# K(4) loaded among the weights of a DeltaNet and SwiGLU kernel, and five smaller edits

## The chip, the cores and the metric

The kernel runs on one core of a Trainium2 chip. The metric is the device time of one execution in microseconds (us). The kernel before was run three times: 692.01, 693.07 and 694.98 us, with the median at 693.07. Engines are named as in the profile: PE is TensorE, PEld its weight loads, DVE is VectorE, ACT is ScalarE, POOL is GpSimd, and SP is the engine that issues most DMAs.

## What is computed

Two blocks, one behind the other. The first is a delta rule over 768 time steps for 4 batches of 8 heads with head dimension 48; the second is a SwiGLU feed-forward block over the 3,072 resulting tokens:

```python
k_n = k / (np.linalg.norm(k, axis=-1, keepdims=True) + 1e-06)
for t in range(S):
    y[:, :, t] = np.einsum('bhd,bhde->bhe', q[:, :, t], state)
    v_old = np.einsum('bhde,bhd->bhe', state, kt)
    state = state + bt[:, :, :, None] * np.einsum('bhd,bhe->bhde', kt, vt - v_old)
...
g = x @ w_gate                      # 384 x 1536
silu = g * (1.0 / (1.0 + np.exp(-g)))
out = (silu * (x @ w_val)) @ w_out  # 1536 x 384
```

Queries, keys, values and beta are 32-bit floats; the three weight matrices come as 64-bit floats and are made 32-bit ones on the chip.

## The kernel before

**Chunks.** Time is cut into 12 chunks of 64 steps. Within a chunk the recurrence becomes matrix products: Gram products of the keys, a triangular inverse, products with the state, and a new state. `advance(c)` is a generator that takes chunk c through these in steps; each `next` issues one step on all engines. The result of a chunk is transposed into `xts[c]`, the 256 tokens that the feed-forward block reads. For chunk 0 the last steps are y (products of L1175, copies L1184 to L1192), x (transposes L1206, copies L1209 and L1210) and the state (`of_state`, L1145).

**Keys, queries, values.** K(c), q(c) and v(c) are the loads of one chunk, each 384 KB in 192-byte runs: two DMAs for K and q (L140), four for v (L186). There are four buffers for keys, so K(4) reuses that of K(0) and is issued at the end of chunk 0's state step (`rows_freed_by`). There are two buffers each for q and v. `turned` transposes keys or queries on TensorE (L511) and copies them back on ScalarE; `gram_steps` (L527) makes the Gram products. `products(4, 2)` does both for K(4) and q(2), with unread products ahead of them (`small_unread`, L658: tiny products whose result nobody reads).

**Weights.** They come in 42 pieces. Pieces 0 to 23 have 256 columns (256 KB, gate and value in turn: even numbers are gate), 24 to 29 have 512 columns (512 KB), 30 to 41 are rows of the output weight (384 KB). `stage(n, after)` issues the load of a piece on SP (L260) into a place that is borrowed from buffers not yet in use; for the early ones a one-element GpSimd copy (L259) holds it until the piece three numbers earlier has landed. A later piece is staged as soon as the piece whose place it takes has been converted (`freed_by`). A piece goes through two ScalarE instructions (`power_step`, L272 and L278) and three on VectorE (`convert`: L289, L297, L309); `convert(ns, ahead)` also runs the powers of some pieces ahead. Each engine works in program order, so a power whose piece has not landed holds all ScalarE work behind it.

**Order.** The whole schedule is by hand: each engine's queue is in the order of the program text. In the first part the pairs (c, f) for the chunks c = 0 and 1 and the column blocks f = 0, 2, ..., 10 go in this order: (0,0), (0,2), (0,4), (0,6), (1,0), (1,2), (1,4), (1,6), (0,8), (1,8), (0,10), (1,10). `gate_val(c, f)` makes the gate product (12 matmul records of L1409), its silu (ACT L1418), the value product and their product h (DVE L1420). The gate and the value product have one PSUM bank each of four, in turn. During (0,0) and (0,2) `chain(at)` is called behind each quarter: it takes a step of `advance` of chunk 0 or 1 and converts one or two pieces. From (0,4) on `fill` converts pieces behind the silu and behind h, and `point` puts in other chunk work: ahead of (0,4) the transposes of K(4) and q(2), ahead of (0,6) their Gram products, whose copies are L553 and L556 on ScalarE. At (1,0) the inverse of the second pair of chunks starts (L856, L569, L860). From chunk 2 on a faster scheme with fewer products runs to the end.

On SP the order around the change is: pieces 18 to 22, q(2), v(2), K(4), piece 23, piece 29, v(3), piece 24, K(5), pieces 25, 26, 28, 27.

Of the kernel before, what the change touches and what calls it, by code (L numbers as in the profile page):

```python
# [20 lines left out]
def kernel(  # L21
# [25 lines left out]
    nc = tc.nc  # L47
# [4 lines left out]
    NB = B // 2  # L52
# [97 lines left out]
    def load_q(c):  # L150
        load_heads(qpad[c % QB], q, c)
# [28 lines left out]
    def load_v(c):  # L180
        vin[c] = work.tile([128, 2, NB, NJ, D], FP32, name="vin", bufs=2)
        for b in range(2):
            src = halves(v, c, b).rearrange("bp (j par) p d -> par p (bp j) d", par=2)
            for par in range(2):
                s = 64 * (b ^ par)
                nc.sync.dma_start(  # L186
                    out=vin[c][s : s + 64, par].rearrange("p bp j d -> p (bp j) d"),
                    in_=src[par],
                )
# [87 lines left out]
        )  # L277
        nc.scalar.activation(power, words_of[:, :, 0], ACTF.Copy, scale=2.0**-29)  # L278

    def convert(ns, ahead=6):  # L280

        work_of = []
        for n in ns:
            dst, _, t, f0, m = pieces[n]
            power_step(n)
            place = staged.pop(n)[:, 0:m]
            work_of.append((dst[:, t, f0 : f0 + m].bitcast(U32), place, powers.pop(n)))
        for dst, place, _ in work_of:
            nc.vector.tensor_scalar(  # L289
                out=place,  # L290
                in0=dst,
                scalar1=3,
                scalar2=None,
                op0=ALU.logical_shift_left,
            )
        for dst, place, _ in work_of:
            nc.vector.scalar_tensor_tensor(  # L297
                out=dst,
                in0=dst,
                scalar=0x80000000,  # L300
                in1=place,
                op0=ALU.bitwise_and,
                op1=ALU.bitwise_or,
            )
        for n in range(ns[-1] + 1, ns[-1] + 1 + ahead):
            if n < min(N_HALF, len(pieces)) or ns[-1] + 3 > n < len(pieces):
                power_step(n)
        for dst, _, power in work_of:
            nc.vector.tensor_tensor(out=dst, in0=dst, in1=power, op=ALU.add)  # L309
        for n in ns:  # L310
            for later in freed_by.get(n, ()):
                stage(later)
# [635 lines left out]
    def advance(c):  # L948
# [100 lines left out]
                skip_group_check=True,  # L1049
            )  # L1050
        if c == 0:
            nc.vector.tensor_copy(v0[:, 0], p_u[:, 0])
            nc.scalar.copy(v0[:, 1], p_u[:, 1])
        elif c == 1:
            flat = v0.rearrange("p par bp j d -> p (par bp j d)")
            for bank in range(2):
                p = p_u_of[bank].rearrange("p par j d -> p par (j d)")
                nc.scalar.copy(by_bank(flat, bank), p)
            v_flat = qpad[1].rearrange("p bp h d -> p (bp h d)")[:, 0 : HH * D]
            v1 = v_flat.rearrange("p (par bp j d) -> p par bp j d", par=2, bp=NB, j=NJ)  # L1060
            crossed_copies(other_half(v_flat), other_half(flat))
            nc.scalar.copy(v1[:, :, 0], v0[:, :, 0])
        else:
            nc.scalar.copy(v0, p_u)
# [54 lines left out]
                    if n + par < 3:  # L1119
                        yield MORE  # L1120
        if c + 2 < NCH:
            if c < 2:
                load_v(c + 2)
            else:
                late_loads.append(lambda: load_v(c + 2))
        yield
        pq = p_sb.pop(c)
# [78 lines left out]
                nc.tensor.transpose(p, y_f[:, bp, at], ident)  # L1206
        x_v = xts[c].rearrange("p t (bp n) -> p t bp n", bp=NB)
        if c == 0:
            nc.scalar.copy(x_v[:, :, 0], p_f[0])  # L1209
            nc.vector.tensor_copy(x_v[:, :, 1], p_f[1])  # L1210
        else:
            nc.scalar.copy(x_v, p_f)
        if 2 <= c < NCH - 1 and (c + 1) // 2 in n_t:
# [400 lines left out]

    todo = list(range(len(pieces)))

    def converts(n):
        if todo:
            convert(todo[:n])
            del todo[:n]  # L1620

    def converts_first(*ns):
# [20 lines left out]
    def products(k_c, q_c):  # L1643

        if k_c == AHEAD:
            small_unread(40)
        if k_c is not None:
            turned(k_c, False)
        if q_c is not None:
            turned(q_c, True)  # L1650
        yield
        if k_c is not None:
            gram(k_c, False, None, (nc.scalar.copy, nc.scalar.copy))
            if k_c % 2 == 1:
                fills.append((k_c // 2, invert(k_c // 2)))
        if q_c is not None and q_c < MERGED:
            gram(q_c, True)
        yield
# [103 lines left out]
    with tc.manual_schedule(  # L1762
# [16 lines left out]
        load_q(1)  # L1779
        load_v(0)  # L1780
        copy_a = nc.scalar.copy
        small_unread(48)
        unread(2)
        turned(0, False, 0)
        p_g = [first_gram(0, "px")]
# [33 lines left out]
        first_z()  # L1819
        some, others = slice(0, HH // 2), slice(HH // 2, HH)  # L1820
        spread_z(0, 1, nc.scalar, some)
        for n in range(18, 23):
            stage(n, n - 3)
        load_q(QB)
        spread_z(0, 0, nc.vector)
        spread_z(0, 1, nc.vector, others)
        scale_v(0)
# [5 lines left out]
        next(first_q[1])  # L1833
        for x in range(2):
            spread_z(1, x, nc.scalar)
        for n in (2, 4, 1, 3, 5, 6, 7):
            power_step(n)
        for _ in range(6):
            step("advance", advance, 0)
        converts_first(0)  # L1840
        step("advance", advance, 0)
        converts_first(2)
        p_n = banks("p_n", "px")
        n_products(1, p_n, (0,))
# [4 lines left out]
        converts_first(5)  # L1849
        scale_v(1)  # L1850
        n_copies_1(p_n, zb_1.rearrange("p k i -> p (k i)"))

        def chain(at):

            step("advance", advance, 0 if steps("advance", 0) < 4 else 1)
            converts((1, 2, 2, 1)[at])

        pairs = [(c, f) for c in range(2) for f in range(0, 8, 2)]
        pairs += [(c, f) for f in range(8, FT, 2) for c in range(2)]
# [65 lines left out]
```

## Time and profile before

| | us |
|---|---|
| median of three runs | 693.07 |
| the profiled execution | 694.12 |
| its span, first to last instruction | 692.4 |
| PE busy | 675.3 |
| DVE busy | 414.2 |
| ACT busy | 262.9 |
| POOL busy | 193.1 |

The page cuts the span into 40 slices of 17.3 us and gives the busy share of each engine in tenths (9 is 90% or more), the clock that TensorE was granted, and the share of the DMA engines:

```
PE   8897999999999999999999999999999999999997
DVE  7898489798666765647456546655555534433342
ACT  4785576213543533344323245232143242142230
PEclk9999899999999999999999999999999999999999
DMA  9667925007561621464333364243243221221210
```

The first four slices hold the loads, the first chunks and the first columns of the weights; from the fifth on TensorE is full. In the timelines below, a row has the start and the length in us, engine, line, operation, tiles and count, and in brackets the idle time before it and what ended it. A row can stand for several instructions, and its length then reaches from the first start to the last end.

### The profile page before, as it was taken

The page shows a single profiled execution, that of the slowest core. Times are in us where ns is not written, and L with a number is a line of the kernel's source. Part 1 is how long each engine was busy: PE and PEld are TensorE (multiplying, and loading weights), DVE is VectorE, ACT ScalarE, POOL GpSimd, SP SyncE. Part 2 cuts the span into 40 slices and gives each one's busy share as a digit, 9 for nine tenths or more (in the row PEclk, how much of TensorE's full clock was granted, in tenths as well). Part 3 has the DMA queues.
Part 4 walks back from the last instruction along what each step waited for, and adds up shares of the span by engine and source line. Part 5 has one row for each costly group of instructions (what it writes and reads, how often), then busy time and mean ns, then how long its engine had stood idle before and what let it go on. Part 6 is the DMA issues. An engine that isn't in the chain of part 4 may idle for free.

```text
span 692.4 us, 24603 instructions
## 1 busy us (share of the span) xinstructions
PE 675.3 (98%) x10836; PEld 630.0 (91%) x10836; DVE 414.2 (60%) x874; ACT 262.9 (38%) x557; POOL 193.1 (28%) x310
## 2 busy tenths in 40 slices
PE   8897999999999999999999999999999999999997
PEld 4786888756999999999999999999999999999997
DVE  7898489798666765647456546655555534433342
ACT  4785576213543533344323245232143242142230
POOL 5110031105893037820037830208810000000000
PEclk9999899999999999999999999999999999999999
DMA  9667925007561621464333364243243221221210
GB/s 133 160 177 180 257 69 161 1 24 163 134 121 25 114 81 40 97 113 93 78 87 71 70 128 81 55 97 83 55 109 69 56 63 47 55 62 46 70 46 24
DMA packets 143850, 62.24 MB, mean 90 GB/s; under 512 B 122976, under 2 KB 126048, under 8 KB 143744
## 3 DMA queue, kind: packets, MB, share of 16 engines
q1 hardware_dynamic: 141536, 60.19, 37.6%
q8 instruction: 85, 1.39, 0.9%
q10 hardware_dynamic: 2080, 0.39, 0.4%
q14 instruction: 21, 0.17, 0.1%
q0 software_dynamic: 128, 0.10, 0.1%
HBM read 53.58 MB, written 7.08 MB: 88 GB/s over the span
## 4 chain that ended last, share of the span: by engine, by line
PE 91%; DVE 3%; ACT 2%; DMA 2%; issue 1%; SPq 0%; DVEq 0%; ACTq 0%
PE ffn L1313 42%; PE ffn L1519 20%; PE ffn L1409 9%; PE ffn L1436 4%; DMA kn<-in_k_dram 2%; PE p_px L977 2%; PE p_py L960 2%; PE p_px L1043 2%; PE p_py L1133 2%; PE p_px L1145 1%; PE p_px L527 1%; PE p_py L1206 1%; PE ffn L1072 1%; PE p_px L921 1%; PE p_py L935 1%
## 5 line engine op out<-in xcount | busy, mean ns | idle before, releaser
L1313 PE MATMUL ffn<-x_ffn,wg_sb 128*128 128x128 f32 x840 | 128.5, 276 | 0.5 <-ACT ffn L1369 0.3
L1313 PE MATMUL ffn<-x_ffn,wv_sb 128*128 128x128 f32 x840 | 128.2, 275 | 0.0
L1313 PEld LDWEIGHTS ffn<-x_ffn,wg_sb 128*128 128x128 f32 x840 | 111.1, 192 | 1.0 <-ACT ffn L1369 0.7
L1313 PEld LDWEIGHTS ffn<-x_ffn,wv_sb 128*128 128x128 f32 x840 | 110.7, 192 | 0.0
L1348 DVE TENSOR_TENSOR h_f<-sil,ffn 128x256 f32<-128x256 f32 x120 | 49.7, 418 | 83.2 <-ACT sil L1343 81.8
L1343 ACT ACTIVATE sil<-ffn 128x256 f32<-128x256 f32 x120 | 45.8, 383 | 128.5 <-PE ffn L1313 126.4
L1519 PE MATMUL ffn<-wo_sb,h_f 128*128 128x192 f32 x480 | 83.4, 328 | 0.0
L860 POOL TENSOR_TENSOR n_b<-mb,half 128x32 f32<-128x32 f32 x5 | 30.0, 6006 | 183.6 <-DVE mb L569 183.6
L1519 PEld LDWEIGHTS ffn<-wo_sb,h_f 128*128 128x128 f32 x480 | 78.1, 190 | 0.3
L599 POOL TENSOR_TENSOR tmp<-zb,mb 128x31 f32<-128x31 f32 (+15 forms) x124 | 68.6, 553 | 16.9 <-DVE mb L586 7.5
L605 POOL TENSOR_TENSOR zb<-zb,tmp 128x31 f32<-128x31 f32 (+15 forms) x124 | 70.0, 565 | 9.7
L1480 DVE TENSOR_TENSOR ffn<-ffn,p_sb 128x512 f32<-128x512 f32 x58 | 40.4, 696 | 49.1 <-ACT ffn L1369 47.7
L1313 PE MATMUL ffn<-x_t,h_f 128*128 128x128 f32 x480 | 61.0, 280 | 0.2 <-ACT ffn L1326 0.2
L1313 PEld LDWEIGHTS ffn<-x_t,h_f 128*128 128x128 f32 x480 | 56.3, 192 | 2.1 <-ACT ffn L1326 0.3
L1480 DVE TENSOR_TENSOR o_sb<-o_sb,ffn 128x192 f32<-128x192 f32 x49 | 17.2, 352 | 64.1 <-PE ffn L1519 61.5
L1326 ACT COPY ffn<-ffn 128x512 f32<-128x512 f32 x30 | 17.1, 571 | 60.8 <-PE ffn L1313 60.8
L1477 DVE TENSOR_TENSOR h_f<-h_f,h_f 128x256 f32<-128x256 f32 x60 | 29.4, 493 | 11.8 <-PE ffn L1519 10.5
L1519 PE MATMUL ffn<-last_k,h_f 128*128 128x192 f32 x200 | 36.0, 327 | 0.0
L1409 PE MATMUL ffn<-x_ffn,wg_sb 128*128 128x256 f32 x144 | 34.4, 385 | 0.3 <-DVE x_ffn L1210 0.3
L1409 PE MATMUL ffn<-x_ffn,wv_sb 128*128 128x256 f32 x144 | 33.8, 382 | 0.0
L1519 PEld LDWEIGHTS ffn<-last_k,h_f 128*128 128x128 f32 x200 | 32.9, 190 | 0.1
L1409 PEld LDWEIGHTS ffn<-x_ffn,wg_sb 128*128 128x128 f32 x144 | 26.7, 191 | 4.6 <-DVE wg_sb L309 0.8
(323 smaller groups left out, 1123.9 us busy)
## 6 DMA issues: line engine op xcount, KB each, us to landing
h_f<-w_s SPq DMA_DIRECT2D x60, 256.0 KB, 2.8
p_sb<-w_s SPq DMA_DIRECT2D x27, 256.0 KB, 2.8
vin<-in_v_dram SPq DMA_DIRECT2D x48, 96.0 KB, 3.4
out_dram<-o_sb SPq DMA_DIRECT2D x48, 96.0 KB, 2.2
kn<-in_k_dram SPq DMA_DIRECT2D x20, 192.0 KB, 4.6
zt<-in_moe_w_out_dram SPq DMA_DIRECT2D x6, 384.0 KB, 3.9
qpad<-in_q_dram SPq DMA_DIRECT2D x36, 64.0 KB, 3.3
w_s<-h_f SPq DMA_DIRECT2D x7, 256.0 KB, 3.5
```

Source lines behind the costliest of these rows:

```text
L599: engine.tensor_tensor(out=t_v, in0=zb[:, 0 : j + 1, j : j + 1].to_broadcast([128, j + 1, m]), in1=mb[:, j : j + 1, j + 1 : R].to_broadcas ...
L605: engine.tensor_tensor(out=zb[:, 0 : j + 1, j + 1 : R], in0=zb[:, 0 : j + 1, j + 1 : R], in1=t_v, op=ALU.add,)
L860: nc.gpsimd.tensor_tensor(out=n, in0=mb.rearrange("p j i -> p (j i)")[:, 0 : R * R : R + 1], in1=half, op=ALU.pow,)
L1313: nc.tensor.matmul(p[:, u], w(u), moving, start=start and u == 0, stop=True, skip_group_check=True,)
L1326: nc.scalar.copy(p_y, p_x)
L1343: nc.scalar.activation(sil[:, n].rearrange("p (i n) -> p i n", i=2), p[:, 0:2], ACTF.Silu)
L1348: nc.vector.tensor_tensor(out=h_of(c, f, j), in0=sil[:, n].rearrange("p (i n) -> p i n", i=2), in1=p[:, 2:4], op=ALU.mult,)
L1409: nc.tensor.matmul(ps[name][:, i], w_sb[:, t, (f + i) * 128 : (f + i + 1) * 128], xts[c][:, t], start=(t == 0 and i == 0), stop=(t == KT - 1),
L1436: nc.tensor.matmul(p_o, hs[c, f - f % 2][:, f % 2, bp * 128 : (bp + 1) * 128], wo_sb[:, f], start=(f == 0), stop=(f == FT - 1),)
L1477: nc.vector.tensor_tensor(out=out, in0=a, in1=b, op=ALU.subtract)
L1480: nc.vector.tensor_tensor(out=out, in0=a, in1=b, op=ALU.add)
L1519: nc.tensor.matmul(p[x, part], a(f - f % 2)[:, f % 2], b(f), start=not begun and f == 0, stop=f == FH - 1, skip_group_check=True,)
```

## The change

K(4) comes directly behind piece 19 on SP: the loads of pieces 20, 21, 22 and q(2) move from the text ahead of chunk 0's steps into the first `chain` call, behind the state step that issues K(4). v(2) is loaded together with v(3), at chunk 1's step. Nine of the 40 unread products ahead of K(4)'s transposes go to the head of the kernel (48 become 57). The first copy of chunk 0's u, on VectorE, is cut into two halves; both copies of chunk 0's x are on ScalarE, where one was on VectorE. The powers of pieces 6 and 7 are issued later, the addition of piece 0 stands behind the y step, and `chain` runs ahead over other numbers of pieces (`CHAIN`: pieces to convert, pieces ahead).

```diff
-    def convert(ns, ahead=6):
+    def convert(ns, ahead=6, between=None):
...
+        if between is not None:
+            between()
         for n in range(ns[-1] + 1, ns[-1] + 1 + ahead):
...
         if c == 0:
-            nc.vector.tensor_copy(v0[:, 0], p_u[:, 0])
+            for bp in range(NB):
+                nc.vector.tensor_copy(v0[:, 0, bp], p_u[:, 0, bp])
             nc.scalar.copy(v0[:, 1], p_u[:, 1])
...
         if c + 2 < NCH:
-            if c < 2:
-                load_v(c + 2)
-            else:
+            if c == 1:
+                load_v(2)
+                load_v(3)
+            elif c > 1:
                 late_loads.append(lambda: load_v(c + 2))
...
         if c == 0:
-            nc.scalar.copy(x_v[:, :, 0], p_f[0])
-            nc.vector.tensor_copy(x_v[:, :, 1], p_f[1])
+            for bp in range(NB):
+                nc.scalar.copy(x_v[:, :, bp], p_f[bp])
...
-    def converts(n):
+    def converts(n, ahead=6):
         if todo:
-            convert(todo[:n])
+            convert(todo[:n], ahead)
             del todo[:n]
...
         if k_c == AHEAD:
-            small_unread(40)
+            small_unread(31)
...
-        small_unread(48)
+        small_unread(57)
...
-        for n in range(18, 23):
+        for n in range(18, 20):
             stage(n, n - 3)
-        load_q(QB)
...
-        for n in (2, 4, 1, 3, 5, 6, 7):
+        for n in (2, 4, 1, 3, 5):
             power_step(n)
         for _ in range(6):
             step("advance", advance, 0)
-        converts_first(0)
-        step("advance", advance, 0)
+        convert([0], 0, lambda: step("advance", advance, 0))
+        todo.remove(0)
+        power_step(6)
         converts_first(2)
...
         n_copies_1(p_n, zb_1.rearrange("p k i -> p (k i)"))
+        power_step(7)
+
+        later_pieces = list(range(20, 23))
+
+        CHAIN = [(1, 5), (2, 3), (2, 6), (1, 6)] + [(n, 6) for n in (1, 2, 2, 1)]
 
         def chain(at):
 
             step("advance", advance, 0 if steps("advance", 0) < 4 else 1)
-            converts((1, 2, 2, 1)[at])
+            if later_pieces:
+                for n in later_pieces:
+                    stage(n, n - 3)
+                later_pieces.clear()
+                load_q(QB)
+            converts(*CHAIN.pop(0))
```

## The prediction

> **What bounds the kernel now.** I read the page first, then the chain of waits for the first 110 us, then the granted clock by stretches, and last the timelines of single engines.
>
> ```profile
> PE 675.3 (98%) x10836; PEld 630.0 (91%) x10836; DVE 414.2 (60%) x874; ACT 262.9 (38%) x557; POOL 193.1 (28%) x310
> ...
> PE 91%; DVE 3%; ACT 2%; DMA 2%; issue 1%; SPq 0%; DVEq 0%; ACTq 0%
> ```
>
> TensorE is busy 98% of the span and holds 91% of the chain that ended last. Only what keeps TensorE waiting, or what it does without need, can move the end. The chain names one DMA, with 2%. In the order of time (start, length, what), with the stretch around it:
>
> ```profile
> 43.52 1.12 PE p_px L1145 x64
> ...
> 62.08 1.51 PE ffn L1409 x6
> 63.59 0.55 SPq L140
> ...
> 64.18 6.36 DMA kn<-in_k_dram
> ...
> 70.67 1.94 PE p_px L511 x8
> ...
> 74.25 5.18 PE ffn L1409 x24
> ...
> 82.56 27.46 PE ffn L1409 x126
> ```
>
> Here K(4), the fifth chunk's keys, lands at 70.54, and the transposes of L511 wait for it. From 82.56 to 110.02 TensorE then has one unbroken run. What the wait costs beside the idle time shows in the stretches (PE, PEld, DVE, ACT, POOL busy; granted clock; DMA share; GB/s):
>
> ```profile
> 65.70:67.20 1.50, 0.00 (x1) 0.00 (x0) 1.28 (x6) 0.10 (x1) 0.00 (x0) 1.00 0.69 131
> 67.20:70.67 3.47, 0.00 (x0) 0.03 (x1) 1.61 (x5) 0.00 (x0) 0.00 (x0) 0.50 1.05 287
> 70.67:74.05 3.38, 3.38 (x16) 3.38 (x17) 0.00 (x0) 1.83 (x4) 0.00 (x0) 0.50 0.59 85
> 74.05:80.00 5.95, 5.95 (x67) 5.06 (x69) 0.46 (x1) 2.79 (x5) 0.00 (x0) 1.00 1.11 259
> ```
>
> TensorE is idle from 65.70 to 70.67, 4.97 us, and 1.5 us into it the clock drops to half until 74.05. The two sets of transposes take 3.4 us in that stretch.
>
> **The change: K(4) moved.** SP's timeline (start, time on the queue, what):
>
> ```profile
> 52.47 0.38 SPq L260 DMA_DIRECT2D wo_sb<-in_moe_w_val_dram  x1
> 52.94 0.38 SPq L260 DMA_DIRECT2D zt<-in_moe_w_gate_dram  x1
> ...
> 58.25 1.32 SPq L140 DMA_DIRECT2D qpad<-in_q_dram  x2
> 59.68 2.97 SPq L186 DMA_DIRECT2D vin<-in_v_dram  x4
> 62.77 2.24 SPq L140 DMA_DIRECT2D kn<-in_k_dram  x2
> 65.13 0.64 SPq L260 DMA_DIRECT2D zt<-in_moe_w_val_dram  x1
> ...
> 66.64 3.69 SPq L186 DMA_DIRECT2D vin<-in_v_dram  x4
> 70.44 3.00 SPq L260 DMA_DIRECT2D wo_sb<-in_moe_w_gate_dram  x1
> ...
> 74.95 1.63 SPq L260 DMA_DIRECT2D wo_sb<-in_moe_w_val_dram  x1
> ```
>
> The row at 52.47 is piece 19, 52.94 piece 20, then 21 and 22, q(2), v(2), K(4), piece 23, (29), v(3), 24, (K(5)) and 25. Afterwards the order is 19, K(4), 20, 21, 22, q(2), 23, 29, v(2), v(3), 24, K(5), 25. K(4) needs the state product of chunk 0 (L1145, done at 44.64), so nothing holds it after 52.85. With its own 2.24 us of issue and the 6.36 us of its slow second half it would land near 60.5, and with twice that transfer at 67; the transposes want it at 65.4 (below). I take 60.5: hidden. GpSimd's one-element copies for 20 to 22 keep their order. These three pieces move by about 1.5 us on SP's queue; they are converted only behind 66.1, so this lies in cover.
>
> How early TensorE could then be, from its own rows:
>
> ```profile
> 17.16 1.04 PE L511 MATMUL p_py<-ident,kn 128*128 128x128 f32 x8
> 18.04 1.04 PE L511 MATMUL p_px<-ident,last_k 128*128 128x128 f32 x8
> ...
> 64.51 0.30 PE L658 MATMUL p_px<-half 32*32 32x1 f32 x16
> 65.00 0.70 PE L658 MATMUL p_px<-half 32*32 32x1 f32 x64 [0.19 <-issue]
> ...
> 74.09 2.75 PE L1409 MATMUL ffn<-x_ffn,wg_sb 128*128 128x256 f32 x12
> ```
>
> The 40 unread products run from 64.51 to 65.70, 1.19 us; 31 of them take 0.92, to 65.43. The two sets of transposes at full clock take 0.88 and 1.04 us (the rows of 17.16 and 18.04), so with 0.1 us between them and the next products the gate product of (0, 4) starts at 65.43 + 1.92 + 0.1 = 67.4 in place of 74.09: **6.7 us earlier**. It is 4.97 idle, 1.4 of half clock and 0.3 of unread products. It needs q(2) by 66.3; issued at about 58.25 as before, it has 8 us, and K(4)'s slow half took 6.36, so I count no wait.
>
> **What is late next.** Everything behind is not a matter of TensorE alone. Piece 25 (issued at 74.95) took
>
> ```profile
> wo_sb<-in_moe_w_val_dram SPq DMA_DIRECT2D x1, 512.0 KB, 5.6
> ```
>
> from issue to landing, and ScalarE stood waiting for it. The rows that follow, on ScalarE, VectorE and TensorE:
>
> ```profile
> 80.54 0.71 ACT L272 ACTIVATE wv_sb<-wo_sb 128x512 f32<-128x512 f32 x1 [1.94 <-DMA wo_sb<-in_moe_w_val_dram]
> ...
> 84.59 0.60 ACT L1418 ACTIVATE sil<-ffn 128x512 f32<-128x512 f32 x1 [0.19 <-PE ffn L1409]
> ...
> 92.45 0.60 ACT L1418 ACTIVATE sil<-ffn 128x512 f32<-128x512 f32 x1
> ```
>
> ```profile
> 96.36 0.68 DVE L1420 TENSOR_TENSOR h_f<-sil,ffn 128x512 f32<-128x512 f32 x1
> ```
>
> ```profile
> 97.34 2.75 PE L1409 MATMUL ffn<-x_ffn,wg_sb 128*128 128x256 f32 x12
> ```
>
> ```profile
> 84.59:92.45 7.86, 7.86 (x38) 6.92 (x37) 4.93 (x9) 7.82 (x9) 0.00 (x0) 1.00 0.16 63
> ```
>
> On ScalarE the power of piece 25 stands ahead of the Gram copies of chunk 4 and of the silu of (0, 6) at 84.59; from there ScalarE is full until the silu of (1, 0) at 92.45 (the last row: ACT, the fourth engine, 7.82 of 7.86); VectorE then transposes, converts piece 27 and makes h of (1, 0), done at 97.04. The product at 97.34, (1, 4), reuses the PSUM banks that this h frees: four banks, two to each (chunk, f). So TensorE starts (1, 4) only 0.30 us after the other engines have let it, and ScalarE waited 0.19 on the way. Of this 0.49 I count 0.4 as room, the rest as semaphores. The gain at (1, 4) is thus the smaller of 6.7 and 0.4 + (80.54 − the new landing of piece 25).
>
> When does piece 25 land? Up to it SP has to issue the same 3,712 KB from q(2) on less K(4)'s 384. Bound from the slow side: only K(4)'s place on the queue goes (62.77 to 65.13, 2.36 us) and all else keeps its pace, so 78.2 and a gain of 2.8. Below that: a later landing than 80.5 would need the queues to get slower, and v(2) and v(3) back to back could do that (a rival). Bound from the fast side: the 3,328 KB left go at the 259 GB/s of the stretch from 74.05, 13.2 us from 58.25, so 71.4, and the full 6.7 us come. The rows between: three issues were held by full queues, the four of v(3) by 3.69 − 2.97 = 0.7, piece 24 by 2.7 (0.3 to 0.4 is normal in the rows of 52.47 and 52.94), piece 25 by 1.3. Those holds come from the same transfers behind one another, which stay except for K(4). I let a quarter of the 4.7 go: 78.2 − 1.2 = 77.0, nearer the slow bound since that stretch is the same one. **Gain 0.4 + 3.5 = 3.9 us**; TensorE waits 2.8 us ahead of (1, 4). Behind it all engines stand as they stood at 97.34, and the rest of the span keeps its length.
>
> **The small edits.**
>
> ```profile
> 1.03 1.57 PE L658 MATMUL p_px<-half 32*32 32x1 f32 x96 [1.03 <-DVE half L316]
> 9.07 1.06 PE L511 MATMUL ffn<-ident,kn 128*128 128x128 f32 x8 [0.59 <-DMA kn<-in_k_dram]
> ```
>
> ```profile
> 31.35 1.28 DVE L545 TENSOR_TENSOR p_sb<-ffn,mask_q 128x512 f32<-128x512 f32 x2
> 32.75 0.55 DVE L1480 TENSOR_TENSOR uu<-v,ffn 128x384 f32<-128x384 f32 x1
> ...
> 41.09 0.55 DVE L1210 COPY x_ffn<-ffn 128x384 f32<-128x384 f32 x1
> ```
>
> Nine unread products at the head: 48 of them are 96 rows and 1.57 us, so 0.29 us, hidden by the 0.59 us that TensorE waits for K(1) at 9.07; with that cover gone, 0.29. Splitting chunk 0's first copy lets TensorE begin up to 0.3 us sooner, but the first sum at 32.75 starts as soon as the two masks (31.35 and 1.28 long) are through VectorE, so the round trip keeps its pace: 0, at worst 0.16 of a second instruction. The second x copy off VectorE (41.09, 0.55) lets the first gate product begin some 0.5 us sooner, but its third weight still needs its conversion, now shorter by the copy and longer by the addition moved behind the y copies (0.42): 0.2 us for TensorE. The powers issued later stay on ScalarE in full. These 0.2 us, and any wait for q(2) up to 2.8 us, end in the wait ahead of (1, 4) and are worth nothing in the forecast.
>
> **Sum.** The profiled execution took 694.12 us (692.4 span, 1.7 around it), 1.05 above the median of the runs, 693.07. 694.12 − 3.9 = 690.2; the same step from the median gives **689.2 us**.
>
> **The rivals.**
> *The full step*: the DMA queues drain faster without K(4) in the thick of them, piece 25 lands by 74.2, and nothing holds (1, 4): 693.07 − 6.7 = 686.4. For it: the DMA share of only 0.69 in the stretch from 65.70, with K(4) under way. Against: the three holds from 66.64 on, which have other transfers as their cause.
> *No gain*: holds grow as v(2) and v(3) follow one another with four issues each, and piece 25 lands within 1 us of 80.5; the idle time moves from the transposes to (1, 4): 692.5. For it: all bytes ahead of piece 25 are the same ones. Against: issues at 52.94 and 58.25 are 5.3 us apart with two pieces between them, room that K(4) now fills.
> *The clock drops again*: the 2.8 us wait ahead of (1, 4) halves the clock, as 1.5 us of idling after small products did at 67.20. One stretch of 3.4 us with TensorE busy at half clock costs 1.7: 689.2 + 1.7 = 690.9. Against: here the wait stands behind dense products. The Trainium skill (TensorE: Matmul & The Clock Gate, section What's actually happening) has the clock fall only after at least one idle window of about 3.4 us. By that rule a 2.8 us wait leaves the clock alone; the row at 67.20, where it fell after 1.5 us without products, disagrees with a strict reading, so I keep the case.
> *Slower*: one mechanism, piece 25 behind v(2) and v(3). If eight head transfers in a row fill the queues so that piece 25 lands later than 80.9, TensorE waits at (1, 4) longer than it gained. At 83 that is 2.1 us, and the idle time there, 8.8 us, takes the clock with it, 1.7: 696.9. For it: v(3) and piece 24 together sat 6.7 us on SP already. Against: 384 KB fewer ahead of it since q(2).
>
> **How the numbers follow.** Forecast 0.50 (its own range 687.5 to 690.5, piece 25 between 75.4 and 78.4), full step 0.21, no gain 0.14, clock 0.10, slower 0.05. The range of 8 in 10 reaches from below the full step, 685.8 (0.6 for the spread of the runs), to 692.0, leaving out most of the no-gain and slower cases. A measurement of this kernel tells about 0.5%, 3.5 us, from no change. Faster by more than this, under 689.6: the full step and some 0.36 of the forecast's 0.50: 0.57. Slower by more, 0.05. Within: 0.38.
>
> **What would show it.** K(4) lands before 62, TensorE is not idle between 65 and 67, and the granted clock stays at 1.00 there. The gate product of (0, 4) starts near 67.4. ScalarE waits for piece 25 until about 77, and TensorE is idle some 3 us ahead of (1, 4), near 91 to 94, with h of (1, 0) as its releaser. No idle there means the full step; a landing of piece 25 at 80 means no gain. I am wrong altogether if K(4) still holds L511, or if the wait stands at another place, as with q(2).

## The result, and the profile after

| | before | after |
|---|---|---|
| median of 21 runs each, taken together, us | 693.38 | 691.60 |
| lowest and highest | 691.11 to 695.66 | 689.67 to 694.45 |
| the profiled execution | 694.12 | 691.6 |
| its span | 692.4 | 689.9 |

The ratio of the times is 0.9968, with a 95% interval of 0.9957 to 0.9979: the kernel after is faster by 0.32%, some 2.2 us (the two medians of the table differ by 1.78 us, 0.26%, inside that interval). The 691.60 lies in the predicted range, 2.4 us above the forecast of 689.2, and it is less than the 0.5% that the prediction had as the likeliest class.

From the page of the kernel after, TensorE's busy time, and the chain that ended last by engine:

```profile
PE 673.6 (98%) x10836; PEld 627.9 (91%) x10836; DVE 414.3 (60%) x874; ACT 263.6 (38%) x558; POOL 193.9 (28%) x310
...
PE 87%; ACT 5%; DMA 3%; DVE 2%; issue 2%; SPq 1%; POOL 0%; DVEq 0%; ACTq 0%; POOLq 0%
```

TensorE still bounds it, but its share of the chain went from 91 to 87%, and ScalarE's from 2 to 5%. TensorE's busy time fell by 1.7 us (675.3 to 673.6), which is about what half a clock costs over the 3.38 us of transposes at 70.67 in the kernel before (an estimate: half of 3.38). The three stretches that held K(4)'s wait, in the kernel after (PE, PEld, DVE, ACT, POOL busy; granted clock; DMA share; GB/s):

```profile
65.70:67.20 1.50, 1.50 (x71) 1.35 (x70) 1.24 (x5) 1.19 (x3) 0.00 (x0) 1.00 0.98 310
67.20:70.67 3.47, 3.47 (x24) 3.19 (x22) 2.26 (x8) 2.43 (x6) 0.00 (x0) 1.00 0.76 139
70.67:74.05 3.38, 3.38 (x48) 2.76 (x49) 0.35 (x1) 0.60 (x1) 0.00 (x0) 1.00 0.87 162
```

TensorE is busy throughout and at full clock, where it was idle for 4.97 us and at half clock for 6.8. Next, TensorE's timeline after, at the places to compare, and then the list of all its waits between 60 and 125 us (what waited, for what; us in total, times, longest):

```profile
66.45 1.09 PE L513 MATMUL p_px<-ident,kn 128*128 128x128 f32 x8
...
68.25 2.75 PE L1413 MATMUL ffn<-x_ffn,wg_sb 128*128 128x256 f32 x12
...
78.02 1.99 PE L1413 MATMUL ffn<-x_ffn,wg_sb 128*128 128x256 f32 x8 [1.34 <-DVE wg_sb L311]
...
92.80 2.75 PE L1413 MATMUL ffn<-x_ffn,wg_sb 128*128 128x256 f32 x12
96.44 2.86 PE L1413 MATMUL ffn<-x_ffn,wv_sb 128*128 128x256 f32 x12 [0.89 <-DVE h_f L1424]
...
110.71 2.86 PE L1413 MATMUL ffn<-x_ffn,wg_sb 128*128 128x256 f32 x12 [1.05 <-ACT sil L1422]
```

```profile
PE ffn L1413 <- DVE wg_sb L311: 1.3, 1, 1.3
PE ffn L1413 <- ACT sil L1422: 1.1, 1, 1.1
PE ffn L1413 <- DVE h_f L1424: 0.9, 1, 0.9
PE p_py L1210 <- issue: 0.5, 1, 0.5
```

K(4)'s transposes (66.45) wait for nothing. The gate product of (0, 4) starts at 68.25 in place of 74.09, 5.84 us earlier. Then the lead melts in three waits that the kernel before did not have: 1.34 us inside the gate product of (0, 6), 0.89 ahead of the value product of (1, 4), and 1.05 ahead of the gate product of (1, 8). The same products before and after give the ledger:

| product | before | after | lead, us |
|---|---|---|---|
| gate (0, 4) | 74.09 | 68.25 | 5.84 |
| gate (1, 0) | 86.98 | 82.44 | 4.54 |
| gate (1, 4) | 97.34 | 92.80 | 4.54 |
| value (1, 4) | 99.93 | 96.44 | 3.49 |
| gate (1, 8) | 112.88 | 110.71 | 2.17 |
| end of the span | 692.4 | 689.9 | 2.5 |

From 117 to 400 us the lead stays at 2.1; the last 0.4 come near 400 us and were not followed up. The three waits have their releasers on ScalarE and VectorE, here on ScalarE (first four rows) and VectorE (last two) of the kernel after:

```profile
76.30 0.66 ACT L272 ACTIVATE wg_sb<-wo_sb 128x512 f32<-128x512 f32 x1 [4.66 <-DMA wo_sb<-in_moe_w_gate_dram]
...
80.11 0.66 ACT L272 ACTIVATE wv_sb<-wo_sb 128x512 f32<-128x512 f32 x1 [2.60 <-DMA wo_sb<-in_moe_w_val_dram]
...
91.79 0.60 ACT L1422 ACTIVATE sil<-ffn 128x512 f32<-128x512 f32 x1
...
109.19 0.55 ACT L272 ACTIVATE wo_sb<-staged 128x384 f32<-128x384 f32 x1 [2.08 <-DMA staged<-in_moe_w_out_dram]
```

```profile
77.54 0.42 DVE L311 CUSTOM_DVE_ANT_0 wg_sb<-wg_sb,last_h 128x512 uint16<-128x512 uint16 x1 [1.20 <-ACT last_h L278]
...
95.71 0.68 DVE L1424 TENSOR_TENSOR h_f<-sil,ffn 128x512 f32<-128x512 f32 x1
```

ScalarE stands 4.66 us for piece 24 and 2.60 us for piece 25, which landed at 80.09. Behind 80.11 it is full again up to the silu of (1, 0) at 91.79; h of (1, 0) follows at 95.71, and the value product of (1, 4) starts 0.05 us after it ends. The wait at (0, 6) is another path from piece 24: the addition of piece 22 on VectorE (77.54) stands behind a power in `last_h` that ScalarE issued after the load of piece 24. The one at (1, 8) is a silu that stood behind the power of an output-weight piece (109.19). So all three are ScalarE work in program order behind a load that is late. The loads of pieces 24 and 25 are late for what SP had to issue ahead of them (its timeline after; 56.30 is piece 20, 60.88 piece 23, 62.63 piece 29):

```profile
54.89 1.32 SPq L140 DMA_DIRECT2D kn<-in_k_dram  x2
56.30 0.87 SPq L260 DMA_DIRECT2D zt<-in_moe_w_gate_dram  x1
...
59.45 1.32 SPq L140 DMA_DIRECT2D qpad<-in_q_dram  x2
60.88 1.71 SPq L260 DMA_DIRECT2D zt<-in_moe_w_val_dram  x1
62.63 1.48 SPq L260 DMA_DIRECT2D p_sb<-in_moe_w_val_dram  x1
64.17 6.72 SPq L186 DMA_DIRECT2D vin<-in_v_dram  x8
71.00 0.56 SPq L260 DMA_DIRECT2D wo_sb<-in_moe_w_gate_dram  x1
...
73.08 2.89 SPq L260 DMA_DIRECT2D wo_sb<-in_moe_w_val_dram  x1
```

v(2) and v(3) take 6.72 us of the queue in one piece, and piece 24 follows. Piece 25 was issued at 73.08 in place of 74.95, but stood 2.89 us on the queue, not 1.63, and landed only 0.42 earlier (80.51 before). The load behind the wait at (1, 8) was issued at 104.09, in place of 104.71, and landed at 109.11; it takes the place of a piece that has to be converted first, and the conversions ran only some 0.6 us ahead of those in the kernel before. With both v loads out of the way (e2 below) it was issued at 100.95.

### The profile page after: what moved, and what is told of

It is laid out like the page before. It is cut to its first block, busy times and chain, and to the rows that moved or that the text cites. A ratio compares the mean times of both kernels' runs of the same rounds, so it can differ in the third digit from the quotient of the medians.

```text
span 689.9 us, 24600 instructions
## 1 busy us (share of the span) xinstructions
PE 673.6 (98%) x10836; PEld 627.9 (91%) x10836; DVE 414.3 (60%) x874; ACT 263.6 (38%) x558; POOL 193.9 (28%) x310
## 4 chain that ended last, share of the span: by engine, by line
PE 87%; ACT 5%; DMA 3%; DVE 2%; issue 2%; SPq 1%; POOL 0%; DVEq 0%; ACTq 0%; POOLq 0%
PE ffn L1317 43%; PE ffn L1523 20%; PE ffn L1440 4%; PE ffn L1413 2%; PE p_px L979 2%; PE p_py L962 2%; DMA wo_sb<-in_moe_w_val_dram 2%; PE p_px L1045 2%; PE p_py L1137 1%; PE p_py L1210 1%; PE p_px L1149 1%; PE p_px L529 1%; PE ffn L1075 1%; ACT a_sb L555 1%; PE p_px L923 1%
## 5 line engine op out<-in xcount | busy, mean ns | idle before, releaser
L1481 DVE TENSOR_TENSOR h_f<-h_f,h_f 128x256 f32<-128x256 f32 x60 | 29.5, 494 | 11.7 <-PE ffn L1523 10.5
```

Of the source, the lines that this page charges most:

```text
L1481: nc.vector.tensor_tensor(out=out, in0=a, in1=b, op=ALU.subtract)
```

## The experiments

My theory: the move of K(4) carries the gain, and v(2) and v(3), still ahead of pieces 24 and 25, take a part of it back through ScalarE's order. The rivals: the small edits carry or cost something; or the waits have another cause than these two loads. All ratios are to the kernel before on the same chip, with a 95% interval. The runs e1 to e4 were on one chip, e5 to e8 on a second and e9 to e11 on a third; the kernel before has medians of 693.62, 692.74 and 690.99 us on them.

### The loads alone, with v(2) and v(3) where the change has them (e4_only_k4_moved)

The kernel before, with the change's order of loads and nothing else:

```diff
-            if c < 2:
-                load_v(c + 2)
-            else:
+            if c == 1:
+                load_v(2)
+                load_v(3)
+            elif c > 1:
...
-        for n in range(18, 23):
+        for n in range(18, 20):
             stage(n, n - 3)
-        load_q(QB)
...
+            if later_pieces:
+                for n in later_pieces:
+                    stage(n, n - 3)
+                later_pieces.clear()
+                load_q(QB)
```

> The kernel before with the loads alone moved as in the change (K(4) behind piece 19, pieces 20 to 22 and q(2) behind it, v(2) with v(3)); unread products, copies, powers and conversions as before. Theory A: the loads carry the whole gain, ratio 0.997 within 0.001. Rival E: the small edits carry a part of it, or K(4) is late without them; the ratio is 0.998 or more.

Measured: 691.56 us, ratio 0.9971 (0.9958 to 0.9984), that of the whole change. TensorE's waits from 60 us on are the same three:

```profile
PE ffn L1410 <- DVE wg_sb L309: 1.2, 1, 1.2
PE ffn L1410 <- DVE h_f L1421: 0.8, 1, 0.8
PE ffn L1410 <- ACT sil L1419: 0.6, 1, 0.6
```

Piece 25 landed at 80.92. The loads carry the whole gain and bring the waits; the small edits together are worth nothing that this measurement can tell.

### The unread products back in their place (e1_products_back)

```diff
-            small_unread(31)
+            small_unread(40)
...
-        small_unread(57)
+        small_unread(48)
```

> The changed kernel with the nine unread products back at their old place (48 at the head, 40 ahead of K(4)'s transposes). The profile of the changed kernel shows chunk 0's first copy of u on VectorE at 31.76 us, where before it was at 30.87. Theory A: this 0.9 us is not the products' doing but differs from execution to execution; the ratio to before stays near the 0.997 of the changed kernel, within 0.001. Rival B: nine products more at the head shift TensorE's stream and cost the 0.9 us; then the copy is back near 30.9 and the ratio falls by 0.0013 to about 0.9955.

Measured: 691.14 us, ratio 0.9965 (0.9949 to 0.9980): no difference from the change in the total. But the head of the kernel differs. TensorE's timeline at the same instructions, first of the kernel after, then of this one:

```profile
26.20 1.88 PE L653 MATMUL ffn<-half 128*32 128x512 f32 x4 [1.63 <-ACT a_sb L555]
```

```profile
25.02 1.91 PE L653 MATMUL ffn<-half 128*32 128x512 f32 x4
```

With 57 products at the head TensorE stands still for 1.63 us at L653, with 48 it does not. The releaser named, the copies of L555, is not the cause: in the kernel before the same unread products ran from 23.83 on, while these copies went on until 25.06. The cause is taken up in the last section. The first copy of chunk 0's u, L1055 on VectorE, then starts at 31.76 in the kernel after and at 30.70 here; over seven profiles with 57 products it starts at 32.3 in the mean (31.76 to 33.27), over seven with 48 at 31.4 (30.70 to 32.03). The two ranges overlap. In the total the 0.9 us are not seen; that the waits at (0, 6), (1, 4) and (1, 8), which follow, swallow them is only argued.

### Both v loads behind the weights (e2_v_behind_weights)

```diff
             if c == 1:
-                load_v(2)
-                load_v(3)
+                pass
...
             if c == 1 and f == 0:
+                load_v(2)
+                load_v(3)
                 finish(1)
```

> The changed kernel with v(2) and v(3) loaded behind piece 31 instead of ahead of piece 24 (768 KB in eight issues less ahead of pieces 24 and 25). Theory A: the landing of pieces 24 and 25 (76.28 and 80.09 us) is what TensorE waits for behind (0, 4); they then land 4 to 5 us sooner, the waits of 1.34 us at (0, 6) and 0.89 us at (1, 4) go, and the time is 2 to 3 us under the changed kernel's (ratio to before about 0.993). Rival C: the queue is held by other things than these bytes, the pieces land within 1.5 us of where they did, and the ratio stays at 0.997. Rival D: the conversions on VectorE and the output weight's loads hold from 92 us on; the pieces land early but the ratio falls by less than 0.001.

Measured: 689.68 us, ratio 0.9936 (0.9914 to 0.9959). TensorE's waits from 60 us on, and ScalarE's power of piece 25 and the silu of (1, 0):

```profile
PE p_py L1209 <- ACT y L1195: 1.0, 1, 1.0
PE p_py L1209 <- issue: 0.3, 1, 0.3
```

```profile
75.18 0.67 ACT L272 ACTIVATE wv_sb<-wo_sb 128x512 f32<-128x512 f32 x1 [0.38 <-DMA wo_sb<-in_moe_w_val_dram]
...
88.69 0.60 ACT L1421 ACTIVATE sil<-ffn 128x512 f32<-128x512 f32 x1
```

```profile
62.73 0.44 ACT L272 ACTIVATE wg_sb<-zt 128x256 f32<-128x256 f32 x1 [3.45 <-DMA zt<-in_moe_w_gate_dram]
```

Piece 25 landed at 75.16, 4.9 us earlier than in the change, and all three waits are gone; ScalarE waits 0.38 for the piece. The gain over before doubles, from 0.32 to 0.64%; the two intervals just touch (0.9957 to 0.9959). What is left at L1209, the transposes of chunk 1's y, lies ahead of (0, 4), and it comes from a weight too: the copies of y stand on ScalarE behind the power of piece 20 (the last row, at 62.73), which landed at 62.71. Piece 20 is one of the three that the change put behind K(4). In the kernel before it landed at 57.13, ahead of its power's turn at 58.90; in the kernel after at 61.40, where ScalarE stood 1.80 us for it without making TensorE wait. In six profiles beside this one (e1, e3, e6, e8, e9, e10) TensorE waits 0.2 to 0.8 us for this y.

### Only v(2) behind the weights (e6_v2_behind)

The same with v(2) alone, v(3) staying ahead of piece 24:

```diff
             if c == 1:
-                load_v(2)
                 load_v(3)
...
             if c == 1 and f == 0:
+                load_v(2)
                 finish(1)
```

> Half the dose: the changed kernel with v(2) alone behind piece 31, v(3) at its place ahead of piece 24. Theory A: pieces 24 and 25 land some 2 us sooner (25 near 78), and the ratio lies between 0.9968 and 0.9936, near 0.995. Rival C: it is not the bytes but the place of the issues; then the pieces land where they did (76.3 and 80.1) or as early as with both moved (70.8 and 75.2).

Measured: 689.45 us, ratio 0.9942 (0.9923 to 0.9960). Piece 25 landed at 77.06, between the 75.16 of e2 and the 80.09 of the change, and the three waits are gone. So one load of four DMAs seems to cost piece 25 some 2 to 3 us; this is one profile each, and the kernel after by itself has landings 2.4 us apart (80.09 and 82.47, below). A landing at 77 is early enough here. That is the very time that the prediction gave it with both v loads ahead. In its profiled execution, 692.41 us, the clock was at half from 67.04 to 73.87 us (last section), so the (0, 4) product began late there; this can hide a wait in that one profile, but the twelve runs have the gain.

### The powers of pieces 24 and 25 behind the silu (e3_powers_behind_silu, e5_both)

If ScalarE's order is the link, a power that isn't issued ahead cannot hold the work behind it. On the kernel after:

```diff
             if todo[0] < N_HALF:
-                converts(3)
+                converts(3, 0)
```

> The changed kernel with the powers of pieces 24 and 25 taken from ahead of the additions of pieces 21 to 23 and put behind the silu of (0, 6); no DMA is moved. Theory A: it is ScalarE's order, a power waiting for its piece with the Gram copies and the silu of (0, 6) behind it, that hands the late landing to TensorE; the silu then starts near 78 us instead of 83.96, the waits of 1.34 and 0.89 us go though piece 25 still lands at about 80, and the time is 2 to 3 us under the changed kernel's (ratio to before about 0.993). Rival D: the conversions of pieces 24 to 29 themselves are late and TensorE waits as long at (1, 4) or (0, 8); ratio 0.996 to 0.997.

Measured: 690.15 us, ratio 0.9954 (0.9940 to 0.9969). ScalarE's silu of (0, 6), the power of piece 25, the silu of (1, 0):

```profile
80.93 0.60 ACT L1422 ACTIVATE sil<-ffn 128x512 f32<-128x512 f32 x1 [1.28 <-PE ffn L1413]
...
83.49 0.67 ACT L272 ACTIVATE wv_sb<-wo_sb 128x512 f32<-128x512 f32 x1 [0.85 <-DMA wo_sb<-in_moe_w_val_dram]
...
93.47 0.60 ACT L1422 ACTIVATE sil<-ffn 128x512 f32<-128x512 f32 x1
```

The silu of (0, 6) no longer stands behind piece 25. The silu of (1, 0) does still: it comes 10.0 us after the landing at 83.47 in place of 11.7 (80.09 to 91.79), and TensorE waited 1.1 us for h of (1, 0). The piece landed 3.4 us later than in the change in this execution, so a part of the freedom went there. The order on ScalarE is a link in the chain, but moving these powers alone did not give what was expected (0.993, with both waits gone): it gained 0.46% in all, between the 0.32 of the change and the 0.64 of e2, and its interval overlaps both, so that its own worth is not settled.

e5_both has this edit and e2's together.

> The changed kernel with both: v(2) and v(3) behind piece 31, and the powers of 24 and 25 behind the silu of (0, 6). Theory A: v(2) and v(3) out of the way already takes the landing of pieces 24 and 25 off TensorE's path (their removal alone gave 0.9936, with no wait of TensorE behind 68 us), so the order on ScalarE adds nothing: 0.993 to 0.994. Rival D: conversions still hold something behind (1, 4), which shows as an additional fall by 0.001 or more.

Measured: 689.33 us, ratio 0.9953 (0.9931 to 0.9975). Of the three waits none is left, as in e2, and the time is not better than e2's: with the loads early, the order of the powers has nothing to give.

### Are the unread products needed? (e7_no_unread)

e5 without the 31 products ahead of K(4)'s transposes:

```diff
-        if k_c == AHEAD:
-            small_unread(31)
         if k_c is not None:
```

> Both moves, and the 31 unread products ahead of K(4)'s transposes left out. Theory A: with pieces 24 and 25 off the path every us of TensorE ahead of (0, 4) counts; the products take 0.6 us (rows of 65.83, 0.68 long), so the ratio falls by 0.0009 against both moves alone. Rival F: they keep the clock up at this place (the granted clock fell to half at 66.83 for 3.4 us in the run with v(2) and v(3) behind); without them it falls in more executions, at 1.7 us each, and the ratio rises by 0.001 or more.

Measured: 689.06 us, ratio 0.9945 (0.9926 to 0.9965), against e5's 0.9953 on the same chip: no difference that the intervals can tell. The clock was at 1.00 in the profile of this one.

### Both kernels once more (e8_again, b2_before_again)

The two kernels, unchanged, in a second profiled execution each, to see how far one execution speaks for the rest.

> The changed kernel itself, a second profiled execution. Theory A: chunk 0's first copy of u on VectorE, 31.76 us in the first profile, lies elsewhere between 30.5 and 33.5, as in the four runs with other edits (30.70, 31.89, 33.27, 31.52), while piece 25 again lands near 80 and TensorE waits again at (0, 6) and (1, 4), about 2 us in all. Rival: the copy is at 31.8 again, and the 0.9 us belong to the change.

> The kernel before itself, a second profiled execution: K(4) again lands near 70 and TensorE waits 4 to 6 us for it; chunk 0's first copy of u between 30.6 and 31.5 by theory H. Whether the granted clock falls behind the wait again is open.

The kernel after took 693.2 us there, piece 25 landed at 82.47, and the waits for a silu, an h and a weight add to 3.4 us (1.6, 1.1, 0.7). Of the 1.6 for a silu 0.70 lies ahead of the gate product of (1, 4), a fourth place, which e1 and e3 have too (0.3 each). The kernel before took 690.43 us, on the third chip, and this is TensorE's only wait from 60 us on, and the gate product of (0, 4):

```profile
PE p_px L511 <- DMA kn<-in_k_dram: 0.7, 1, 0.7
```

```profile
70.59 2.76 PE L1409 MATMUL ffn<-x_ffn,wg_sb 128*128 128x256 f32 x12
```

The wait for K(4) was 0.73 us, not 4.97, with no half clock behind it, and (0, 4) began 3.5 us sooner than in the first profile. The expected 4 to 6 us did not come, and the first copy of u was at 32.03, later than the expected 30.6 to 31.5. The bottleneck of the prediction was real in the execution that it was read from, but how large it is differs from one execution to the next, or from chip to chip; two profiles do not tell which.

### The better version (e9_v_behind_48), without the 31 (e10_v_behind_48_0), and the loads alone (e11_loads_alone)

e9 is e2 with 48 unread products at the head in place of 57; e10 is e9 without the 31 of L660; e11 is the kernel before with K(4) moved as in e4, and v(2) and v(3) moved as in e2.

```diff
-                load_v(2)
-                load_v(3)
+                pass
...
-        small_unread(57)
+        small_unread(48)
...
             if c == 1 and f == 0:
+                load_v(2)
+                load_v(3)
                 finish(1)
```

> The changed kernel with v(2) and v(3) behind piece 31 and the nine products taken away at the head (48 there, 31 ahead of K(4)). In all seven profiles with 57 at the head TensorE stood 1.4 to 2.5 us at the two unread products of L653 near 26 us, and chunk 0's first copy of u came at 31.76 to 33.27; in the three with 48 it never stood there, and the copy came at 30.70 to 31.52. Theory H: the nine products cost some 0.9 us there, unseen so long as piece 25 holds TensorE later; with v out of the way it counts, the copy is back at 30.6 to 31.5 and the ratio is about 0.001 under that of the same kernel with 57 (0.9936, and 0.9945 to 0.9953 in its two relatives), so 0.993 to 0.994. Rival: the place of the standstill was chance, or something behind it makes up for it; copy at 31.8 or later, ratio 0.9945 or more.

> As the run with 48 at the head and v(2), v(3) behind, and without the 31 products ahead of K(4)'s transposes. Theory: another 0.6 us, ratio 0.0009 lower. Rival F: the clock falls more often at this place and the ratio is 0.001 or more higher.

> The kernel before with its loads alone moved: K(4) behind piece 19, and v(2), v(3) behind piece 31; products (48 and 40), copies, powers and conversions as before. Theory A with H: this has nearly the whole gain, ratio 0.993 to 0.9945, and no wait of TensorE above 0.5 us behind 67 us. Rival E: the small edits are needed once the loads are out of the way; 0.996 or more.

Measured, six runs each, on one chip:

| kernel | median, us | ratio | interval |
|---|---|---|---|
| e9 | 686.29 | 0.9929 | 0.9911 to 0.9947 |
| e10 | 688.21 | 0.9947 | 0.9930 to 0.9965 |
| e11 | 687.50 | 0.9944 | 0.9928 to 0.9960 |

TensorE's waits from 60 us on, first of e9, then of e11, and e9's row of piece 25 on ScalarE:

```profile
PE p_px L660 <- issue: 0.6, 1, 0.6
PE p_py L1209 <- ACT y L1195: 0.3, 1, 0.3
```

```profile
PE p_px L658 <- issue: 0.2, 1, 0.2
```

```profile
74.17 0.71 ACT L272 ACTIVATE wv_sb<-wo_sb 128x512 f32<-128x512 f32 x1 [1.83 <-DMA wo_sb<-in_moe_w_val_dram]
```

Piece 25 landed at 74.15 in e9 and 73.31 in e11, and no wait of TensorE for a weight, a silu or an h is left in either. e9's interval lies wholly below that of the change (0.9957 to 0.9979), and below that of e1, which differs from it in the place of the v loads and in nine of the 40 products ahead of K(4) (0.9949 to 0.9980, on another chip). The loads alone, e11, have most of it (0.56 of 0.71%). Which of the three is best is not settled: their intervals overlap. So does e9's with e2's, so that the price of the nine products in the total stays open too; e9's first copy of u came at 31.62, just behind the range expected of it. e10 missed its expectation: without the 31 products the ratio was to fall by 0.0009, and it is 0.0018 higher. The rival's reason, a clock that falls more often, does not show: the mean granted clock of e10's six runs is 0.998 to 1.0, that of e9's 0.996 to 1.0. Since the two intervals overlap, there may be no difference at all.

## Why the prediction was right in kind and too high in size

**K(4) hidden, (0, 4) early: right.** K(4) landed at 60.86, with 60.5 predicted; the transposes wait for nothing; the clock stays at 1.00. (0, 4) came 5.84 us earlier, with 6.7 predicted. The rest lies ahead of (0, 4): a standstill of 0.53 at L1210, and the one at L653 (both in the last section).

**What is late next: the right piece and the right engine.** ScalarE waits for piece 25 and holds h of (1, 0), and TensorE waits for that h. It is shown by its dose: piece 25 was issued at 73 to 75 us and landed at 80.1 to 83.5 in the five profiles with K(4) moved and both v loads ahead of piece 25 (the change twice, e1, e3, e4); at 70.7 and 77.1 with one (e6); at 65.1 to 67.4 and 72.7 to 75.2 with none (e2, e5, e7, e9, e10, e11). In the first group TensorE waits for wg, h or silu in each; in the others never, from 60 us on.

**The landing: the term that was mis-sized.** "I let a quarter of the 4.7 go" gave 77.0; it was 80.09, 3.1 us later. Some holds went (piece 24 stood 0.56 us on the queue, not 3.00), but others took their place: q(2) went out at 59.45, not 58.25, pieces 23 and 29 stood 2.2 us longer (1.71 and 1.48 for 0.64 and 0.33), and piece 25 stood 2.89. Without K(4) it was issued 1.87 us sooner, but took 7.01 us to land where the prediction kept 5.57. So of the 3.1 us some 1.7 are a later issue (73.08, where 77.0 less 5.57 gives 71.4) and 1.4 a slower transfer. The bytes of v(2), ahead of K(4) before, came to stand right ahead of piece 24. Taking the v loads away gives the issue back, not the transfer: from issue to landing piece 25 takes 6.3 to 8.1 us in all profiles with K(4) moved, with both v loads ahead, one or none. So the v loads act by the time that they take on SP's queue; why the transfer is slower than before stays open. The second rival, "no gain", had this landing (within 1 us of 80.5), though not the time: it gave 692.5.

**The three pieces behind K(4): moved further than thought.** The prediction has pieces 20 to 22 move by about 1.5 us on SP and finds cover, as they are converted behind 66.1. Piece 20 was issued 3.36 us later (56.30 for 52.94), and what comes first is not its conversion on VectorE but its power on ScalarE, ahead of chunk 1's y. In the profile of the change this cost TensorE nothing, in seven others 0.2 to 1.0 us (e2 above).

**The room: too small, by the wrong bank.** The prediction took the gate product at 97.34 as the one that h of (1, 0) frees, with 0.4 us of room. But the gate's bank is freed by the silu (in e1, e3 and e8 this gate product waits for a silu, not for h), and the product that waits for h is the value product, at 99.93 before. h ended at 97.04 there, so the room was 2.9 us. With the landing as it was, 0.4 us earlier, and an h 0.65 us earlier, the lead at that product became 3.49. The two errors have opposite signs: 0.4 + 3.5 predicted, 2.9 + 0.6 found. That 3.9 came so near 3.49 is luck. By the right room a landing at 77.0 would have kept 2.9 + 3.5 = 6.4 us, all of the lead of 5.84; e6, with its 77.06, gains what e2 gains, which agrees.

**Behind (1, 4) all stands as before: wrong.** The wait at (1, 8) took another 1.3 us (3.49 to 2.17): a silu behind a power of the output weights, for which ScalarE stood until 109.19. That load came no earlier than the late conversions let it, so it may be piece 25's lateness passed on; it was not tested by itself. The wait at (0, 6) was not foreseen either, but it seems to have cost nothing: without it TensorE would have stood longer at the value product of (1, 4).

**The base.** The 6.7 us came from one execution at 694.12 us. In the second the same wait was 0.73 us. The best kernel here, with the lead kept in full, gains 0.71%, 4.9 us (3.7 to 6.2 by its interval), not 6.7: so the full-step rival, 686.4, was too low even for a version in which nothing holds (1, 4).

**The small edits.** Priced at nothing, and nothing was found in the total (e1, e4). But the nine products did have a price where they were put at none. The wait for K(1) at 9.07 went in the kernel after, as predicted, though it is absent in e1 with 48 products too. And a standstill of 1.4 to 2.5 us appeared at L653 in all seven profiles with 57, and in none of the seven with 48. Most of those with 48 stand longer a little later (up to 1.57 us at L1043 or L1045), so that the price at the head is not the whole standstill but the 0.9 us, in the mean, of the copy of u.

**The rivals.** Slower: piece 25 never landed so late that the lead turned: 83.47 at the latest, with a room of 2.9 us beyond 80.5. The clock did not fall behind the waits of 0.9 to 1.3 us.

## What to carry to other kernels

Before a load is moved forward on a queue, list what lands next on each in-order engine, and follow it to the product that reuses the bank it frees; the order of the loads behind is part of the change. Transfers in short runs (v, 192 bytes) that are needed late belong behind the large ones that are needed soon. And a wait of one profiled execution is not the wait of the median: profile the same kernel twice before a sum is built on it.

## What the runs showed of the hardware

**Instruction blocks.** The page of the kernel after has, among the DMA queues (packets, MB, share of 16 engines):

```profile
q8 instruction: 85, 1.39, 0.8%
```

That is 16 KB for each packet, and 85 of them for TensorE's 21,672 instructions: 256 in each. Counted in TensorE's stream, the standstills at the head that outlast the tiles waited for lie at the numbers 705, 961, 1217 and 1473 or one behind, which are 256 apart: in the kernel after at all four (at 961 the copy of `qs` ends at 21.87 and TensorE goes on at 22.47), in the kernel before at the first and the last. At number 1217 the kernel after has the first product of L653 and stands for 1.63 us; one packet of the queue ended at 25.0, and TensorE went on at 26.2. In the kernel before the same number falls 36 instructions later in the program (18 products and their weight loads), behind the long products of L651 (1.9 us for four), and the weight loads lose 0.06 us there. At 705 it is the kernel before that stands longer, 1.40 us, the one after 0.64. The 0.53 us at L1210 belong here too: from 36 to 130 us every standstill that the 14 profiles put down to "issue" is at 2,241, 3,009 or 3,521 or one behind, whole blocks of 256 from 705, and ends 1.2 to 1.7 us behind the end of a packet. That nine products decide where it falls is shown by e1; that the packet is late because the data queues are full is only argued. The Trainium skill (Runtime: NRT & Kernel Launch, section Instruction fetch mechanics) has these blocks of 256 instructions and calls the price of a crossing mostly hidden. The block size agrees with the row. The price was hidden in the kernel before at 1217, with long products ahead of the boundary, and not in the kernel after, where it was 1.63 us.

**The clock.** Apart from the first 9 us and the end of the span, in 11 of the 14 profiles the granted clock was at half for one stretch of 3.41 us or two (6.83), between 17 and 74 us; it began near 17 to 18 us in three of them, near 26 to 27 in three, near 33 in two and near 67 in three. Laid on a grid of 3.41 us that ends at the drop, the stretch ahead of it always had TensorE busy for at most 0.60 of its time (0.28 to 0.60); behind a busier one it never fell. In a profile without a drop the grid is laid on from the time at which the clock rose at the start (6.68 us in the kernel after, 7.48 in e7). Three stretches of such grids, with the one behind each: from e5, from the kernel after, from e7.

```profile
22.61:26.02 3.41, 1.17 (x82) 1.14 (x72) 3.00 (x12) 2.69 (x6) 0.47 (x2) 1.00 0.54 170
26.02:29.44 3.42, 3.20 (x4) 0.47 (x3) 3.38 (x6) 0.79 (x1) 1.16 (x2) 0.50 0.54 153
```

```profile
23.75:27.16 3.41, 1.78 (x58) 1.10 (x51) 3.10 (x10) 2.81 (x7) 0.37 (x2) 1.00 0.56 150
27.16:30.58 3.42, 3.15 (x136) 2.17 (x138) 2.92 (x5) 0.60 (x1) 0.89 (x1) 1.00 0.45 120
```

```profile
24.55:27.96 3.41, 1.50 (x7) 0.41 (x4) 3.21 (x8) 2.66 (x6) 0.18 (x1) 1.00 0.56 163
27.96:31.37 3.41, 3.41 (x187) 2.92 (x188) 2.17 (x4) 0.54 (x2) 1.13 (x2) 1.00 0.47 150
```

With 1.17 us busy of 3.41 the next stretch runs at half clock; with 1.78 and 1.50 it does not, and e6's stretch of 1.68 was followed by half clock, so the busy time alone does not decide it. In e6 the clock stayed at half for a second stretch, though TensorE was busy in all of the first. The drop behind K(4)'s wait in the kernel before belongs here: 1.72 us busy in the 3.42 ahead of 67.22, and not the 1.5 us of idling alone. The Trainium skill (TensorE: Matmul & The Clock Gate, section What's actually happening) has free-running windows of about 3.4 us, which agrees with 3.41 and 6.83; it asks for an idle window, where here one with half its time busy was enough.
